# GpSimd behind VectorE's weight operations, by semaphore; and 21 calls of zero products in place of 30

## The chip, the core and the metric

The kernel runs on one core of a Trainium2 chip. A core has TensorE (matmuls, with their results in PSUM), VectorE, ScalarE and GpSimd (elementwise work and reductions), and SyncE, which here issues the transfers between HBM and SBUF. Each engine executes its own instructions in the order in which they are written; between engines, semaphores order them. The metric is the time on the device of one execution in microseconds, lower is better. Three runs of the kernel before took 982.82, 984.07 and 984.09, median 984.07.

## The reference

Rotary attention over 4 batches, 8 heads, 576 positions and head size 64, then two feed-forward blocks over the 2304 tokens:

```
q_rot, k_rot = rotate(q), rotate(k)          # halves turned by cos, sin of the position
scores = q_rot @ k_rot.T / 8;  attn = softmax(scores, axis=-1)
x = attn @ v                                 # (2304, 512)
h = x @ w_in                                 # (512, 2048)
x = where(h > 0, h, exp(min(h, 0)) - 1) @ w_out
out = ((x @ w1) * (x @ w2)) @ w3 @ w_out2    # inner width 1024
```

All is float32. The weights are handed to the kernel as 64-bit words (the float arrives as two 32-bit halves), which three integer operations on VectorE and one on ScalarE make into float32.

## The kernel before, in words

The kernel has three stages, the attention (up to about 280 us of the trace), the first feed-forward block, and the second one with the output. Products are made as three matmuls of split operands (high times high, high times low, low times high; `PAIRS`).

**The attention.** Two heads of a batch are one unit (`units`, 16 of them). A unit goes through five chunks of query rows (`c` from 0 to 4). For each: TensorE multiplies the scores into PSUM (`score`, L406), two buffers (`ps_s`) that alternate; VectorE takes the negative maximum (`most`, L466); ScalarE takes the exponential into SBUF (`expo_s`, L472), which frees the buffer; TensorE turns the result (`half`, L417), VectorE or ScalarE copies it out of PSUM (L481, L479), and TensorE multiplies it by v (`weigh`, L590). The fifth chunk of a unit holds the last 64 rows of both heads (`scores_4`, products with `diag`).

Beside that run preparations. *Rotary steps* for a later unit: for k (640 columns) and q (576) each two products by the table (L330), a sum (L333), a copy of the high part on ScalarE (L82), and the low part (`low`, L339). They may go to GpSimd or VectorE; in the attention after unit 0 all are on GpSimd. `low` frees the buffer for a further load of q or k by SyncE. *Weights* (`weight_steps`): for each of 16 blocks one operation on ScalarE (L124) and three on VectorE, a shift (L127) and two that combine two inputs (L130, L133), on 128 x 512 integers. *Spreads* (L86 on GpSimd, L82 on ScalarE) of 1/sum, which TensorE turns; *sums* of weights on GpSimd (L165 to L168) and at the end of the attention its parts of the next stage's operands (L185, L193, L148).

**The order.** The class `Plan` writes one list for all engines. Each operation has an engine (or a choice of two), a planned duration, a due time and predecessors; `order()` simulates the engines and yields the operations by planned start, and the loop behind `first_scores()` writes them out in this order. TensorE's operations keep the order in which they were added, the others go by due time among those that can start. GpSimd and the VectorE operations with `lock=True` (the three per weight, and VectorE's rotary steps) share one entry in `free`, so that in the plan neither starts before the other's end, less 0.02 us:

```
if e == "pool" or e == "dve" and ops[i][8]:
    t = max(t, free.get("lock", t) - 0.02)
```

That exclusion is in the plan alone. In the program nothing orders a weight operation and a GpSimd operation on other data.

**The start.** `first_load` fetches the table and the first unit's k and q in parts. Meanwhile TensorE multiplies zeros (`warm_up(WARM)`; a call of a float32 product shows as two matmuls in the trace). `first_rope` makes the first operands on VectorE and ScalarE. `first_scores` multiplies the first chunk's scores in two halves, with `warm_up(FILL_IN)` between them; `FILL` puts further such products ahead of later chunks of unit 0.

Of the kernel before, what the change touches and what calls it, by code (L numbers as in the profile page):

```python
# [31 lines left out]
HOLD_0 = 12.0  # L32
AHEAD = dict(act=0.2, dve=0.2, pool=0.3)
RATHER = {"dve/act": dict(act=0.1), "pool/dve": dict(dve=1.2), "pool/act": dict(act=0.3)}
WARM = 30
FILL = (4, 2, 2, 2, 2)
FILL_IN = 4


PRE = [(z, 2 * q + i) for q in range(3) for z in "io" for i in range(2)] + [("o", 6 + i) for i in range(4)]  # L40
# [19 lines left out]
def kernel(  # L60
    ctx: ExitStack, tc: tile.TileContext, q, k, v, tables, ident, w_in, w_out, w1, w2, w3, w_o2, out
):
    nc = tc.nc
    act, dve, pool, pe = nc.scalar, nc.vector, nc.gpsimd, nc.tensor
# [152 lines left out]
    class Plan:  # L217
# [10 lines left out]
        def order(self):  # L228
            ops, done, free, sent = self.ops, {}, {}, {}
            ops = [o[:6] + (max(o[6], o[3] - self.hold),) + o[7:] if o[0] != "pe" else o for o in ops]  # L230
            need = [[self.at[d] for d in o[5] if d in self.at] for o in ops]
            queues = {}
            for i, o in enumerate(ops):
                for e in o[0].split("/"):
                    queues.setdefault(e, []).append(i)
            for e, q in queues.items():
                if e != "pe":
                    q.sort(key=lambda i: ops[i][3])
            line = EARLY
            while any(queues.values()):  # L240
                best = None
                for e, q in queues.items():
                    found = []
                    for i in q[:1] if e == "pe" else q[:120]:
                        if all(d in done for d in need[i]):
                            t = max([free.get(e, self.start[e]), ops[i][6]] + [sent.get(d, done[d]) if e == "sp" else done[d] for d in need[i]])
                            if e == "pool" or e == "dve" and ops[i][8]:
                                t = max(t, free.get("lock", t) - 0.02)
                            found.append((t + (RATHER[ops[i][0]].get(e, 0.0) if "/" in ops[i][0] else 0.0), ops[i][3], i, t))
                    if not found:  # L250
                        continue
                    t0 = min(found)[0]
                    s, _, i, t = min((f for f in found if f[0] <= t0 + AHEAD.get(e, 0.05)), key=lambda f: f[1])
                    if best is None or s < best[0]:
                        best = s, e, i, t
                assert best, [(e, [(list(self.at)[i], [list(self.at)[d] for d in need[i] if d not in done]) for i in q[:6]]) for e, q in queues.items()]
                _, e, i, t = best
                o = ops[i]
                b = o[1][e] if "/" in o[0] else o[1]
                for e_ in o[0].split("/"):  # L260
                    queues[e_].remove(i)
                free[e] = t + b
                if e == "pool" or e == "dve" and o[8]:
                    free["lock"] = free[e]
                if e == "sp":
                    line = max(line, t + 1.5) + o[2]
                    done[i] = line + 0.7
                    if o[7]:
                        sent[i] = t
                else:  # L270
                    done[i] = t + b + o[2]
                f = o[4]
                yield t, (lambda: f(e)) if "/" in o[0] else f, (e, b), i

    ctx_o = ctx.enter_context(ExitStack())
    ctx_x = ctx.enter_context(ExitStack())
# [3 lines left out]
    with ExitStack() as c1:  # L280
# [118 lines left out]
        def score(i, c, e, n, z):  # L399

            hl = hls[units[i]]
            h = slice(64 * e, 64 * e + 64) if c < 4 else slice(0, P)
            a, b = PAIRS[z]
            w = hl[h, a, c * P:c * P + P] if c < 4 else diag[i % 2][:, a]
            at_ = S + 64 * (1 - e) + 288 * n
            pe.matmul(S_t[i, c, e][:, n, :288], w, hl[h, b, at_:at_ + 288], start=(z == 0), stop=(z == 2))  # L406

        def open_s(i, c, e):
            S_t[i, c, e] = ps_s.tile([P, 2, 512], F32, tag="s", name="s")
# [9 lines left out]
        def first_scores():  # L419
            for e in range(2):  # L420
                open_s(0, 0, e)
            for n in range(2):
                if n:
                    warm_up(FILL_IN)
                for z in range(3):
                    for e in range(2):
                        score(0, 0, e, n, z)
# [243 lines left out]
        for i in range(NU):  # L671
            for c in range(5):
                k_ = ("Pb", i, c) if c < 4 else ("S4", i)
                t = nom[k_] + (0.4 if c < 4 else 0.85)
                for e, name in enumerate("ab" if c < 4 else "4"):
                    x = (i, c) if c < 4 else (i,)
# [9 lines left out]
            for c in range(4):  # L686
                k_ = (i, c + 2) if c < 2 else (i + 1, c - 2)
                free = (("PV", i - 1, 0, 1),) if c < 2 else (("PV", i - 1, 1, 2),)
                EV(("evy", i, c), nom["Pa", *k_] + 1.0, lambda e, i=i, c=c: evacuate(i, c, 1, e), ("Pa", *k_), *free)
                EV(("evx", i, c), nom["Pc", *k_] + 1.0, lambda e, i=i, c=c: evacuate(i, c, 0, e), ("Pc", *k_), *free)  # L690
            t = nom["T4", i] + 0.5
            EV(("ev4", i), t + 1.2, lambda e, i=i: evacuate_4(i, e), ("T4", i), ("PV", i - 1, 1, 2))
            t = nom["l1", i] + 0.5
            OP("dve/act", dict(dve=V_(256) + V_(128), act=A_(256, False) + A_(128, False)))(("evl", i, 1), t + 0.8, lambda e, i=i: evacuate_tails(i, 1, e), ("l1", i), ("PV", i - 1, 1, 1))
            t = nom["r1", i] + 0.5
            OP("dve/act", E_(320))(("evr", i, 1), t + 1.5, lambda e, i=i: evacuate_spread(i, 1, e), ("r1", i))
            t = nom["s0", i] + 0.5
            OP("dve/act", E_(256))(("evl", i, 0), t + 0.4, lambda e, i=i: evacuate_tails(i, 0, e), ("s0", i), ("PV", i - 1, 0, 1))
            OP("dve/act", E_(256))(("evr", i, 0), t + 0.8, lambda e, i=i: evacuate_spread(i, 0, e), ("s0", i), ("evl", i, 0))
            for hf in range(2):  # L700
                dep = ("expb", i, 1) if hf == 0 else ("exp4", i)
                t = nom[("s0", i) if hf == 0 else ("r1", i)]
# [3 lines left out]
                t = nom[dep]  # L706
# [28 lines left out]
        for i in range(1, NU):  # L735
            if i:
                t0 = nom["Pa", i, 0]
                for w in (1, 0):
# [4 lines left out]
                    t = t0 - (7.5, 14.5)[w]  # L743
# [15 lines left out]
        for m, (z, f) in enumerate(PRE):  # L759
            key = (z, f)  # L760
            t = AT_0 + 18.0 + (end - AT_0 - 34.0) / (len(PRE) - 1) * m
# [14 lines left out]
        for n in range(SUMS):  # L776
            t = nom["Pa", 8 + 3 * n, 0]
# [17 lines left out]
        t = nom["Pa", NU - 1, 2]  # L795
# [19 lines left out]
        def warm_up(n):  # L815

            ps = ps_t.tile([P, 512], F32, tag="t", name="warm") if n else None
            for _ in range(n):
                pe.matmul(ps[:, :P], warm, warm, start=True, stop=True)
# [10 lines left out]
        dve.memset(warm, 0.0)  # L830
        warm_up(WARM)
        for d in diag:
# [3 lines left out]
        pool.memset(rb[1][:, 2], 0.0)  # L836
        pool.memset(pl1[64:, 256:], 0.0)
        first_scores()
        for t, fn, o, i in plan.order():
            fn()  # L840
            if PLOG is not None:
                PLOG.append((t, o[0], o[1], list(plan.at)[i]))

# [17 lines left out]
    with ExitStack() as c2:  # L861
# [129 lines left out]
        for n in range(N1 + 1):  # L991
            t = T(n)
            p, f = divmod(n, NQ)
# [98 lines left out]
        for n in range(N1):  # L1092
            due = T(n)
            for q in range(4):
                w = (512, 512, 512, 256)[q]
                free = (LAST_USE[(q - 1) % 4], n - 1 if q else n - 2)
# [31 lines left out]
        for n in range(N1):  # L1128
            for z in (1, 0):
# [3 lines left out]
                free = ("Y3", n - 1) if z else ("Y1", n)  # L1133
# [6 lines left out]
        for p in range(1, NT3):  # L1140
            t = T(p * NQ)
# [56 lines left out]
        for m, w in enumerate(every):  # L1198
# [5 lines left out]
            if w[0] == "e":  # L1204
                if w[1][0] == "h" and w[1][2] == 0:
                    f = w[1][1]
# [36 lines left out]
        t = T(N1)  # L1243
        for j in range(8):
            at_ = O_AT[j]
            free = [("wo", N1 - NQ + WO_AT.index(at_), z) for z in range(2)] if at_ in WO_AT else [("made", *w) for w in early[-3:]]
# [305 lines left out]
```

## Time and profile before

| | |
|---|---|
| median of three runs | 984.07 us |
| profiled execution, its own time | 984.18 us |
| span of its trace | 982.4 us |
| TensorE busy | 959.7 us, 98% |
| VectorE busy | 795.1 us, 81% |
| ScalarE busy | 650.4 us, 66% |
| GpSimd busy | 218.6 us, 22%, all of it in the first 276 us |
| mean granted TensorE clock | 0.997 |

A time in the trace counts from its first instruction. Busy is what an engine spent in instructions; TensorE's matmuls are pipelined and their ends are modelled, so a busy TensorE is not one at its peak. PEclk in a stretch is the mean granted clock, 1.00 being 2.4 GHz and 0.50 being 1.2 GHz. PE is TensorE, PEld its loading of the stationary operand, DVE VectorE, ACT ScalarE, POOL GpSimd, SP SyncE. An entry such as `[1.78 <-POOL hl L339]` says that the engine stood idle for 1.78 us before the instruction, and what ended that. A tile's number is left out of its name. A row of stretches has, after its length, the busy microseconds and the number of instructions of PE, PEld, DVE, ACT and POOL, then the clock, the share of the DMA engines and GB/s; a unit's stretch runs from the start of one unit's first product with `diag` to that of the next.

### The profile page before, as it was taken

The numbers are of one execution on the slowest core, as the hardware profiler recorded it, in microseconds if no ns is written. First come the engines' busy times: TensorE is split into PE (matmuls) and PEld (weight loads), VectorE is DVE, ScalarE is ACT, GpSimd is POOL, SyncE is SP. The second block draws the span as 40 slices with busy tenths as digits, with TensorE's granted clock in tenths as the row PEclk, the third lists the DMA queues.
The fourth block names the chain that finished last, engine by engine and source line by source line (L and its number), as shares of the span: only waits on it lengthen the run. The fifth ranks groups of instructions, "written<-read, shape, count | busy, mean of one in ns | idle before, by whom it ended". The sixth has DMA issues, their size and how long they took to land.

```text
span 982.4 us, 17951 instructions
## 1 busy us (share of the span) xinstructions
PE 959.7 (98%) x6652; PEld 833.0 (85%) x6652; DVE 795.1 (81%) x1499; ACT 650.4 (66%) x1393; POOL 218.6 (22%) x190
## 2 busy tenths in 40 slices
PE   8899999999999999999999999999999999999998
PEld 7676676666779999999999999988899999999997
DVE  5899899999879999999999999847656666676444
ACT  4687787767778787888788877865344444444342
POOL 4999998886510000000000000000000000000000
PEclk9999999999999999999999999999999999999999
DMA  6444443442403356476655676614232342224201
GB/s 212 162 145 138 147 130 138 153 136 79 165 3 116 122 192 205 160 229 226 193 188 155 196 246 202 220 44 150 66 95 76 87 139 76 75 91 147 81 27 64
DMA packets 62536, 134.54 MB, mean 137 GB/s; under 512 B 6640, under 2 KB 15472, under 8 KB 62448
## 3 DMA queue, kind: packets, MB, share of 16 engines
q1 hardware_dynamic: 62448, 133.39, 42.3%
q8 instruction: 52, 0.85, 0.3%
q14 instruction: 36, 0.29, 0.1%
HBM read 107.68 MB, written 25.69 MB: 136 GB/s over the span
## 4 chain that ended last, share of the span: by engine, by line
PE 71%; DVE 3%; ACT 1%; DMA 1%; issue 1%; ACTq 0%; DVEq 0%
PE y L923 12%; PE A L1353 10%; PE o L1379 10%; PE A L880 9%; PE B L1353 7%; PE B L880 7%; PE yb L924 6%; PE w L1283 4%; PE o L590 2%; PE s L406 2%; DMA set<-kept 1%; PE ptp L417 1%; DVE set L141 0%; DVE xc L78 0%; ACT pr L472 0%
## 5 line engine op out<-in xcount | busy, mean ns | idle before, releaser
L923 PE MATMUL y<-g,wo 128*128 128x512 f32 x576 | 204.1, 392 | 0.0
L924 PE MATMUL yb<-g,wo 128*128 128x256 f32 x576 | 161.2, 280 | 0.0
L141 DVE TENSOR_TENSOR set<-set 128x512 fp32r<-128x512 f32 (+1 forms) x160 | 98.2, 619 | 40.4 <-ACT set L138 40.2
L406 PEld LDWEIGHTS s<-hl 64*128 64x128 f32 x768 | 86.9, 185 | 46.3 <-ACT pr L472 32.4
L472 ACT ACTIVATE pr<-s,nm 128x576 f32<-128x576 f32 x144 | 105.5, 738 | 31.1 <-DVE nm L466 30.1
L923 PEld LDWEIGHTS y<-g,wo 128*128 128x128 f32 x576 | 107.8, 187 | 20.4
L406 PE MATMUL s<-hl 64*128 64x288 f32 x768 | 108.8, 315 | 12.8 <-ACT pr L472 10.9
L1353 PE MATMUL A<-xc,set 128*128 128x384 f32 x576 | 116.1, 336 | 0.2
L466 DVE TENSOR_REDUCE nm<-s 128x1 f32<-128x576 f32 x144 | 102.7, 748 | 12.2 <-PE s L406 11.9
L880 PE MATMUL A<-xf,set 128*128 128x384 f32 x552 | 111.2, 336 | 0.8 <-ACT p L937 0.7
L1379 PE MATMUL o<-W,g 128*128 128x512 f32 x432 | 111.1, 393 | 0.0
L1353 PEld LDWEIGHTS A<-xc,set 128*128 128x128 f32 x576 | 102.3, 188 | 7.8 <-DVE p L1440 1.0
L924 PEld LDWEIGHTS yb<-g,wo 128*128 128x128 f32 x576 | 108.7, 189 | 0.1
L880 PEld LDWEIGHTS A<-xf,set 128*128 128x128 f32 x552 | 93.7, 188 | 4.1 <-ACT p L937 1.4
L82 ACT ACTIVATE g<-p 128x384 fp32r<-128x384 f32 x48 | 25.2, 525 | 107.8 <-DVE p L1440 71.5
L330 POOL TENSOR_TENSOR raw_qk<-raw_qk,tab 128x640 f32<-128x640 f32 (+1 forms) x60 | 90.7, 1523 | 3.2 <-DMA raw_qk<-q_ 2.9
L1379 PEld LDWEIGHTS o<-W,g 128*128 128x128 f32 x432 | 80.0, 188 | 12.7
L138 ACT ACTIVATE set<-set 128x512 fp32r<-128x512 f32 (+1 forms) x160 | 89.3, 567 | 1.9 <-DMA set<-kept 1.7
L1353 PE MATMUL B<-xc,set 128*128 128x384 f32 x432 | 86.5, 334 | 0.0
L417 PE MATMUL ptp<-idt,pr 64*128 64x64 f32 x1024 | 86.3, 226 | 0.0
L880 PE MATMUL B<-xf,set 128*128 128x384 f32 x420 | 84.3, 336 | 0.0
L417 PEld LDWEIGHTS ptp<-idt,pr 64*128 64x128 f32 x1024 | 76.9, 139 | 0.9 <-DVE nm L466 0.5
(248 smaller groups left out, 1833.7 us busy)
## 6 DMA issues: line engine op xcount, KB each, us to landing
set<-kept SPq DMA_DIRECT2D x120, 256.0 KB, 2.8
raw<-w_ SPq DMA_DIRECT2D x32, 512.0 KB, 4.1
kept<-wr SPq DMA_DIRECT2D x40, 256.0 KB, 3.2
raw_qk<-k_ SPq DMA_DIRECT2D x15, 640.0 KB, 5.5
raw_qk<-q_ SPq DMA_DIRECT2D x15, 576.0 KB, 4.7
raw<-w_in_ SPq DMA_DIRECT2D x16, 512.0 KB, 5.8
raw<-w_out_ SPq DMA_DIRECT2D x16, 512.0 KB, 5.0
w<-kept SPq DMA_DIRECT2D x24, 256.0 KB, 3.1
```

Of the source, the lines that this page charges most:

```text
L138: act.activation(t[:, 0, :w], t[:, 1, :w].bitcast(F32), ACTF.Copy)
L141: eng.tensor_tensor(t[:, 1, :w], t[:, 1, :w].bitcast(F32), t[:, 0, :w].bitcast(F32), op=ALU.subtract)
L330: eng.tensor_tensor(r[:, z], r[:, z], tab[:, w, z, TAB[w]], op=ALU.mult)
L406: pe.matmul(S_t[i, c, e][:, n, :288], w, hl[h, b, at_:at_ + 288], start=(z == 0), stop=(z == 2))
L417: pe.transpose(pts[i, c, z][:, e, kc], pr[h, at_:at_ + P], idt[h, h])
L466: dve.tensor_reduce(nm_t[i, c, e], S_t[i, c, e][:, :, :288], axis=AX.XY, op=ALU.max, negate=True)
L472: act.activation(pr_t[i, c][:, e].rearrange("p (n i) -> p n i", n=2), S_t.pop((i, c, e))[:, :, :288], ACTF.Exp, bias=nm_t.pop((i, c, e)), ...
L880: pe.matmul(banks[b][:, :HF], set_w(n, k, a, c), x[:, e, c], start=(start and i == 0), stop=i == 5, skip_group_check=True,)
L923: pe.matmul(y_t[p, o], w_, g[:, c, :512], start=s, stop=t, skip_group_check=True)
L924: pe.matmul(yb_t[p, o // 2][:, o % 2], w_, g[:, c, 512:], start=s and o % 2 == 0, stop=t, skip_group_check=True,)
L1353: pe.matmul(ps[:, :HB], w[:, a, c * P:(c + 1) * P], x[:, c, b], start=(start and i == 0), stop=i == 5, skip_group_check=True,)
L1379: pe.matmul(outs[p, o], g[:, a, o % 3 * P:o % 3 * P + P], wW[f][:, c], start=(f == 0 and i == 0), stop=(f == NG - 1 and i == 2),)
```

## The change

The plan's exclusion is written as two rules without the 0.02 us: a GpSimd operation starts no earlier than the end of the last locked VectorE operation (`BEHIND[0]` is added, 0.0), and a locked VectorE operation no earlier than the end of the last GpSimd operation (`BEHIND[1]`, 0.0). `order()` also yields whether an operation is locked.

In the loop that writes the list out, the last instruction of each locked VectorE operation is remembered. The first GpSimd instruction of the next GpSimd operation in the list is then made dependent on it, so it waits by semaphore for that VectorE instruction's end. One GpSimd operation waits, those behind it follow in GpSimd's own order. No wait is added on VectorE.

Apart from that, `WARM` goes from 30 calls to 21 and `FILL_IN` from 4 to 6.

```diff
--- before.py
+++ after.py
@@ -32,9 +32,10 @@
 HOLD_0 = 12.0
 AHEAD = dict(act=0.2, dve=0.2, pool=0.3)
 RATHER = {"dve/act": dict(act=0.1), "pool/dve": dict(dve=1.2), "pool/act": dict(act=0.3)}
-WARM = 30
+BEHIND = (0.0, 0.0)
+WARM = 21
 FILL = (4, 2, 2, 2, 2)
-FILL_IN = 4
+FILL_IN = 6
 
 
 PRE = [(z, 2 * q + i) for q in range(3) for z in "io" for i in range(2)] + [("o", 6 + i) for i in range(4)]
@@ -244,8 +245,10 @@
                     for i in q[:1] if e == "pe" else q[:120]:
                         if all(d in done for d in need[i]):
                             t = max([free.get(e, self.start[e]), ops[i][6]] + [sent.get(d, done[d]) if e == "sp" else done[d] for d in need[i]])
-                            if e == "pool" or e == "dve" and ops[i][8]:
-                                t = max(t, free.get("lock", t) - 0.02)
+                            if e == "pool":
+                                t = max(t, free.get("by_dve", t) + BEHIND[0])
+                            if e == "dve" and ops[i][8]:
+                                t = max(t, free.get("pool", t) + BEHIND[1])
                             found.append((t + (RATHER[ops[i][0]].get(e, 0.0) if "/" in ops[i][0] else 0.0), ops[i][3], i, t))
                     if not found:
                         continue
@@ -260,8 +263,8 @@
                 for e_ in o[0].split("/"):
                     queues[e_].remove(i)
                 free[e] = t + b
-                if e == "pool" or e == "dve" and o[8]:
-                    free["lock"] = free[e]
+                if e == "dve" and o[8]:
+                    free["by_dve"] = free[e]
                 if e == "sp":
                     line = max(line, t + 1.5) + o[2]
                     done[i] = line + 0.7
@@ -270,7 +273,7 @@
                 else:
                     done[i] = t + b + o[2]
                 f = o[4]
-                yield t, (lambda: f(e)) if "/" in o[0] else f, (e, b), i
+                yield t, (lambda: f(e)) if "/" in o[0] else f, (e, b, o[8]), i
 
     ctx_o = ctx.enter_context(ExitStack())
     ctx_x = ctx.enter_context(ExitStack())
@@ -836,8 +839,21 @@
         pool.memset(rb[1][:, 2], 0.0)
         pool.memset(pl1[64:, 256:], 0.0)
         first_scores()
+        behind = None
         for t, fn, o, i in plan.order():
+            traced = nc.cur_bb.bb.instructions
+            n = len(traced)
             fn()
+            if o[0] == "pool" and behind:
+                mine = [x for x in nc.cur_bb.bb.instructions[n:] if x.engine == behind[1]]
+                if mine:
+                    tc.add_manual_dep(
+                        mine[0], behind[0], mybir.DependencyInfo(mybir.DependencyClass.Sync, mybir.DependencyReason.DATA),
+                        reason="behind",
+                    )
+                    behind = None
+            elif o[0] == "dve" and o[2]:
+                behind = nc.cur_bb.bb.instructions[-1].name, mybir.EngineType.Pool
             if PLOG is not None:
                 PLOG.append((t, o[0], o[1], list(plan.at)[i]))
```

## Rows read from the trace of the kernel before

**Rows 1.** Stretches, one per unit: length, busy us of each engine, TensorE clock
```profile
26.69:44.31 17.62, 15.67 (x169) 11.17 (x167) 14.81 (x26) 13.05 (x31) 15.50 (x14) 0.90 0.42 149
...
124.25:140.03 15.78, 15.38 (x178) 10.94 (x174) 14.08 (x28) 13.18 (x33) 13.85 (x12) 1.00 0.42 139
...
188.49:203.81 15.32, 15.14 (x175) 10.90 (x173) 14.04 (x28) 11.92 (x30) 14.52 (x14) 1.00 0.41 142
203.81:222.12 18.31, 15.88 (x173) 10.99 (x173) 17.30 (x29) 12.22 (x32) 13.60 (x11) 1.00 0.45 149
...
238.82:254.24 15.42, 15.19 (x173) 10.92 (x174) 15.01 (x32) 10.95 (x26) 5.48 (x8) 1.00 0.09 28
...
sum 243.14, PE 231.22 PEld 164.35 DVE 221.74 ACT 184.71 POOL 203.04; mean PE 15.41 PEld 10.96 DVE 14.78 ACT 12.31 POOL 13.54
```

**Rows 2.** Waits, 28 to 262 us: who, releaser, total us, times, longest
```profile
PEld s L406 <- ACT pr L472: 30.5, 54, 2.1
ACT pr L472 <- DVE nm L466: 24.9, 30, 1.7
```

**Rows 3.** Groups on VectorE, 28 to 262 us: busy us, mean ns, idle before
```profile
L133 DVE SCALAR_TENSOR_TENSOR pair<-raw,pair 128x512 int32<-128x512 int32 x16 | 17.8, 1112 | 0.0
L130 DVE SCALAR_TENSOR_TENSOR pair<-raw,pair 128x512 int32<-128x512 int32 x16 | 14.9, 930 | 0.0
L127 DVE TENSOR_SCALAR pair<-pair 128x512 int32<-128x512 int32 x16 | 14.0, 873 | 0.0
```

**Rows 4.** Single lines, whole kernel: least/median/most ns, first and last start
```profile
L127 DVE TENSOR_SCALAR pair<-pair x32: 384/420/1709, 29.9 to 375.6; 128x512 int32<-128x512 int32 x32
L130 DVE SCALAR_TENSOR_TENSOR pair<-raw,pair x32: 654/684/2027, 34.0 to 380.5; 128x512 int32<-128x512 int32 x32
L133 DVE SCALAR_TENSOR_TENSOR pair<-raw,pair x32: 658/685/1934, 37.4 to 383.0; 128x512 int32<-128x512 int32 x32
```

**Rows 5.** Timeline, GpSimd beside VectorE, two pairs: start us, duration us, what
```profile
53.26 2.12 POOL L333 TENSOR_TENSOR raw_qk<-raw_qk 128x576 f32<-128x576 f32 x1
53.43 0.68 DVE L130 SCALAR_TENSOR_TENSOR pair<-raw,pair 128x512 int32<-128x512 int32 x1
...
204.07 1.55 POOL L330 TENSOR_TENSOR raw_qk<-raw_qk,tab 128x640 f32<-128x640 f32 x1
204.14 2.03 DVE L130 SCALAR_TENSOR_TENSOR pair<-raw,pair 128x512 int32<-128x512 int32 x1
```

**Rows 6.** Timeline: last rotary step (units 2, 7), first score (unit 2)
```profile
42.84 1.40 POOL L339 TENSOR_TENSOR hl<-raw_qk,hl 128x576 fp32r<-128x576 f32 x1
46.52 0.40 PE L406 MATMUL s<-hl 64*128 64x288 f32 x1
...
109.52 3.39 POOL L339 TENSOR_TENSOR hl<-raw_qk,hl 128x640 fp32r<-128x640 f32 x2
```

**Rows 7.** Timeline, 0 to 30 us; in brackets idle before, releaser
```profile
1.04 9.81 PE L819 MATMUL warm<-warm 128*128 128x128 f32 x60 [1.04 <-DVE warm L830]
...
8.88 0.43 DVE L375 SCALAR_TENSOR_TENSOR hl<-raw_qk,hl 128x256 fp32r<-128x256 f32 x1
...
11.42 0.89 DVE L359 TENSOR_TENSOR raw_qk<-raw_qk,tab 128x320 f32<-128x320 f32 x2
...
13.17 0.76 DVE L466 TENSOR_REDUCE nm<-s 128x1 f32<-128x576 f32 x1 [0.87 <-PE s L406]
...
15.19 0.49 DVE L375 SCALAR_TENSOR_TENSOR hl<-raw_qk,hl 128x320 fp32r<-128x320 f32 x1 [0.19 <-ACT hl L82]
...
15.76 0.65 POOL L86 TENSOR_SCALAR diag<-hl 64x128 fp32r<-64x128 f32 x2 [13.57 <-DVE hl L375]
...
19.26 0.69 ACT L124 ACTIVATE pair<-raw 128x512 f32<-128x512 f32 x1 [0.41 <-DMA raw<-w_in_]
...
29.84 0.18 PEld L406 LDWEIGHTS s<-hl 64*128 64x128 f32 x1 [1.78 <-POOL hl L339]
```

**Rows 8.** Two microseconds of the products of zeros; columns as in rows 1
```profile
8.00:10.00 2.00, 2.00 (x20) 2.00 (x19) 1.95 (x5) 0.42 (x1) 0.00 (x0) 1.00 1.02 385
```

## The prediction

> **What bounds the kernel now.** I read the busy shares by stage first (only the attention, up to about 280 us, has GpSimd at work, and there TensorE idles), then cut the attention into its 16 units, which are the period of its list. The cuts are the starts of the products with `diag` that close a unit. A unit is 16.21 us on the mean (243.14 / 15), but units 7, 11 and 14 take 15.78, 15.32 and 15.42, mean 15.51, and unit 12 takes 18.31 [rows 1]. The long unit is long on VectorE: 17.30 us busy with 29 instructions, against 14.04 with 28 in unit 11, while TensorE has the same 173 to 178 matmuls in each. The waits tell how that reaches TensorE: scores wait for the exponentials that free their PSUM buffer (30.5 us), and the exponentials wait for the maxima on VectorE (24.9 us) [rows 2]. VectorE executes in the order of its list, so whatever delays one of its instructions delays the next maximum.
>
> What delays it are the three operations per weight. 16 of each form run in the attention with means of 873, 930 and 1112 ns [rows 3]; the same forms have medians of 420, 684 and 685 ns over all 32, the half behind the attention included, where GpSimd is silent [rows 4]. The excess is 16 x (0.453 + 0.246 + 0.427) = 18.0 us. One of them can be watched: GpSimd starts a rotary product at 204.07, VectorE its operation at 204.14, and this takes 2.03 us, 1.35 over its median, ending 0.55 behind the product's end at 205.62 [rows 5].
>
> I went through all 48 operations so, with the list in hand: 19 of them carry 16.2 of the 18.0 us, and in each of these the GpSimd operation that held VectorE up stands behind the weight operation in the list and ran past it. The other 1.8 us come from GpSimd operations that stand ahead of it.
>
> **The waits.** 44 of the 48 weight operations have a GpSimd operation behind them before the next weight operation; the last few, where GpSimd has little to do, share one. So some 44 waits are added, all on GpSimd. Behind a waiting instruction stand the rest of GpSimd's list: rotary steps, whose last one (`low`, L339) the next unit's scores need, the spreads of 1/sum (L86), which the turned sums on TensorE need, and two sums of weights. SP's loads of q and k wait for `low` too.
>
> What VectorE gets back: the 19 stalls, 16.2 / 18.0 = 0.9 of the excess, if nothing comes in their place. What that is worth is read from the units, not from 18.0 us: leaving out unit 1 and the three undisturbed ones, 11 units take 243.14 - 17.62 - 46.52 = 179.0 us, against 11 x 15.51 = 170.6. So 8.4 us of the attention's length go with the stalls. The rest of the 18.0 us is covered already (VectorE has room in most units).
>
> What GpSimd pays: in 21 pairs the later operation started before its weight operation would have ended; summed over them (weight operation's start plus its unblocked time, minus GpSimd's start) it is 24.7 us, over 44 waits 0.56 each. The hand-over adds 0.08 us, as from VectorE's end at 15.19 + 0.49 = 15.68 to GpSimd's start at 15.76 [rows 7]. So about 0.6 us per wait, three waits a unit. GpSimd's own pace is read from `low` of q: it ends at 44.24 for unit 2 and for unit 7, as the second of the row's two operations, at 109.52 + 3.39 = 112.91: 68.67 / 5 = 13.73 us a unit [rows 6]. With 3 x 0.6 it is 15.5, just the undisturbed pace of TensorE. It fits with no room, and the slack at the beginning is small: unit 2's `low` ends at 44.24 and its first score runs at 46.52 [rows 6].
>
> So not all of it is gained. Where VectorE comes early, it now meets the GpSimd operation ahead of it in the list; where it comes late, GpSimd stands and its next operations are late. I let a third of the gain go for that: 8.4 x 0.9 x 2/3 = 5.0 us, between 0 (every stall comes back from the operation ahead) and 8.4; below nothing only by GpSimd as pacemaker, below. I lean to the upper half since the list itself is written as if the two excluded each other, so a wait in it mostly restores the order that was meant.
>
> A rule of the Trainium skill (SBUF — State Buffer, section "Who interferes with whom") says that an operation with two SBUF inputs and a GpSimd operation that reads SBUF take one port pair in turn, and the second to start is blocked for the whole of the first. The 2.03 us of rows 5 agree; in the other pair there GpSimd begins at 53.26, VectorE 0.17 later, and yet VectorE runs its plain 0.68 us while the add on GpSimd takes 2.12, against 1.40 for an operation of its size in rows 6. So within 0.2 us the starts do not tell the winner. By the rule taken alone a wait only picks the loser and the gain would be 0.
>
> Unit 1 is 17.62 us, 2.1 over, but its TensorE also stood 1.78 us for `low` at 29.84 [rows 7] and ran at a mean granted clock of 0.90, so partly at 1.2 GHz [rows 1]. Of its 2.1 I take 0.3, between 0 and 2.1.
>
> **The plan's arithmetic.** The old form let either engine start 0.02 us before the other's end, the new one does not. That can turn single choices of order; I cost it at 0 and leave ±1 us for it, about a unit's usual scatter (15.32 to 15.78 undisturbed).
>
> **The products of zeros.** 30 calls are 60 matmuls from 1.04 to 10.85 [rows 7]. Nine calls fewer are 18 matmuls at the end of the row, where 20 stand in 2.00 us [rows 8]: 1.8 us, so they end at about 9.05. The first scores' last operand is there at 8.88 + 0.43 = 9.31. They run then some 1.5 us earlier, and two more calls of filling put back 4 x 0.10 = 0.4 us before the second half. The maximum that began at 13.17, 0.87 us idle before it, can start when VectorE is free: 11.42 + 0.89 = 12.31 [rows 7]. That is 0.86 us. But ScalarE already waited 0.41 us for a weight's load at 19.26 [rows 7], and a load does not come earlier with TensorE; exponentials stand behind it. GpSimd's chain, which sets 29.84, does not pass there until it needs ScalarE's high parts. I take 0.4 us, between 0 and 0.86. The clock rose while the old products ran and 42 are left of 60, so I expect it to rise at the same time.
>
> **Sum.** 5.0 + 0.3 + 0.4 = 5.7 us. Behind the attention nothing changes, and its first products wait for TensorE's own last ones, so the gain is kept. The profiled execution took 984.18 us, its span 982.4 and 1.8 around it; that is 0.1 above the median. 984.18 - 5.7 = 978.5, and against the median 978.4.
>
> **Rivals.**
> *GpSimd becomes the pacemaker* (slower). Today's units leave it (16.21 - 13.73) / 3 = 0.83 us per wait. Beyond that every unit from 2 on waits for `low`. At 1.0 us a unit is 16.73: 0.52 x 13 units = 6.8, less the 2.3 us of slack: +4.5, about 988. For it: the small slack in units 2 and 3, and the spreads, which stand in GpSimd's line. Against it: 0.6 is what the pairs give, and the slack is larger from unit 5 on.
> *The stall changes sides* (about the same). VectorE, now earlier, meets the operation ahead each time and loses as much as before. Only the start's 0.4 is left: 983.7. For it: the rule above; half of a 1.55 us operation is 0.78, more than today's mean of 18.0 / 48 = 0.375. Against it: each wait also brings the two back into step.
> *All of it comes back*: 8.4 + 2.1 + 0.86 = 11.4 us, 972.7. Against it: GpSimd's 15.5 us a unit.
> *The waits don't do it*: the list turns out in another order, with the stalls elsewhere: 984 ± 3.
>
> **Chances.** Forecast (975.5 to 981.5) 0.55; all of it 0.08; changes sides 0.17; pacemaker 0.12; another order 0.08. A difference of under 0.2%, 2.0 us, cannot be told from no change here. Faster: 0.55 + 0.08 + 0.05 of the changed sides + 0.04 of the other order = 0.72; same 0.14; slower 0.12 + 0.02 = 0.14. For 8 in 10 the range takes the forecast, most of the changed sides and the nearer part of the full gain: 974.5 to 985.
>
> **What would show it.** Right: the three weight operations fall to means under 0.75 us in the attention, GpSimd's waits name `pair` of VectorE, units come to 15.5 to 15.9, the first maximum starts near 12.3. Wrong: GpSimd's `low` is what scores wait for in units 2 to 6 (pacemaker), or the means of rows 3 stay while the GpSimd operation that blocks is the one ahead (changed sides), or the start's gain is gone at 19.26.

## The result, and the profile after

The changed kernel takes 973.99 us (median of four runs, 972.47 to 975.60) against 983.87 for the kernel before, measured beside it (median of four, 982.82 to 984.09): 0.9902 of it, interval 0.9880 to 0.9923. I had forecast 978.4 and a range down to 974.5. The direction is right, and the gain is 9.9 us instead of 5.7.

The profiled execution took 972.47 us, its span is 970.7. The stretches of the units, cut as in [rows 1] and with the same columns:

```profile
25.83:42.08 16.25, 14.11 (x168) 10.46 (x166) 13.65 (x26) 12.37 (x30) 14.55 (x12) 1.00 0.41 150
...
119.81:135.11 15.30, 15.29 (x173) 11.00 (x174) 14.68 (x29) 11.65 (x28) 13.44 (x15) 1.00 0.44 144
...
181.55:196.81 15.26, 15.09 (x174) 10.90 (x174) 13.71 (x30) 12.16 (x29) 13.50 (x13) 1.00 0.40 143
196.81:212.74 15.93, 15.56 (x173) 10.99 (x173) 14.62 (x28) 12.70 (x33) 13.55 (x11) 1.00 0.49 171
...
228.21:243.55 15.34, 15.16 (x174) 10.90 (x174) 15.05 (x32) 11.22 (x26) 5.48 (x9) 1.00 0.08 27
...
sum 232.94, PE 227.14 PEld 163.41 DVE 216.39 ACT 181.25 POOL 197.61; mean PE 15.14 PEld 10.89 DVE 14.43 ACT 12.08 POOL 13.17
```

Here the difference of the two spans, 982.4 - 970.7 = 11.7 us, can be shared out. Unit 1 now ends at 42.08 instead of 44.31: 2.2 us. Units 2 to 15 take 232.94 - 16.25 = 216.69 instead of 243.14 - 17.62 = 225.52: 8.8 us. The rest behind the attention gives 0.6, which is scatter (it lies between 710.9 and 713.5 us in the fourteen profiles of this study). Unit 12, which was 18.31, is 15.93: VectorE is busy for 14.62 us in it instead of 17.30, with one instruction less. The medians over all fifteen units are no longer pulled up by a few long ones.

The waits that answer to [rows 2], 28 to 262 us, and the largest groups of the new ones, on GpSimd (who, releaser, total us, times, longest):

```profile
PEld s L409 <- ACT pr L475: 24.9, 57, 1.1
ACT pr L475 <- DVE nm L469: 12.8, 18, 1.5
...
POOL rb L87 <- DVE ri L560: 5.4, 3, 3.4
...
POOL xs L186 <- DVE pair L134: 5.3, 1, 5.3
POOL raw_qk L333 <- DVE pair L131: 5.0, 8, 0.6
...
POOL hl L342 <- DVE pair L128: 2.6, 3, 1.7
POOL rb L87 <- DVE pair L131: 2.5, 4, 0.6
POOL raw_qk L333 <- DVE pair L134: 2.5, 4, 0.6
POOL raw_qk L333 <- DVE pair L128: 2.4, 5, 0.9
...
PEld s L409 <- POOL hl L342: 1.4, 1, 1.4
```

The exponentials wait half as long for maxima (12.8 us instead of 24.9). GpSimd now waits for `pair`, mostly for 0.4 to 0.9 us at a time; one of the waits ahead of `low` (`hl`, L342) takes 1.7 us, and the one of 5.3 us stands at the end of the attention, ahead of the next stage's operands (L186). The scores wait for GpSimd's `low` once, in unit 1, as before.

The weight operations that answer to [rows 3]:

```profile
L131 DVE SCALAR_TENSOR_TENSOR pair<-raw,pair 128x512 int32<-128x512 int32 x16 | 15.2, 950 | 0.0
L134 DVE SCALAR_TENSOR_TENSOR pair<-raw,pair 128x512 int32<-128x512 int32 x16 | 14.5, 907 | 0.0
L128 DVE TENSOR_SCALAR pair<-pair 128x512 int32<-128x512 int32 x16 | 9.7, 607 | 0.0
```

Against the medians of [rows 4] 16 x (0.266 + 0.222 + 0.187) = 10.8 us of excess are left of 18.0. So the operations are still held up, and yet most of the time is gained. Which ones are left is seen in a stretch of VectorE and GpSimd (start, duration, idle before):

```profile
72.67 1.56 POOL L336 TENSOR_TENSOR raw_qk<-raw_qk 128x640 f32<-128x640 f32 x1
...
73.07 1.71 DVE L131 SCALAR_TENSOR_TENSOR pair<-raw,pair 128x512 int32<-128x512 int32 x1
...
74.86 1.41 POOL L333 TENSOR_TENSOR raw_qk<-raw_qk,tab 128x576 f32<-128x576 f32 x1 [0.63 <-DVE pair L131]
```

GpSimd's operation of 72.67 stands ahead of the weight operation in the list, VectorE comes 0.40 us after it began and stands until 0.55 us behind its end: the picture of [rows 5], with the other neighbour. The next GpSimd operation waits and starts 0.08 us after VectorE's end, 73.07 + 1.71 = 74.78. In all 48 operations, with undisturbed times of 0.40, 0.67 and 0.67 us, what is left comes from a GpSimd operation ahead, none from one behind. Before, 12 of them were held up for more than 0.8 us each, 13.6 us together; now 2, with 2.1 us.

The start, answering to [rows 7]:

```profile
1.04 6.33 PE L822 MATMUL warm<-warm 128*128 128x128 f32 x42 [1.04 <-DVE warm L833]
...
8.56 0.86 PE L409 MATMUL s<-hl 64*128 64x288 f32 x6 [1.19 <-ACT hl L83]
...
11.88 0.75 DVE L469 TENSOR_REDUCE nm<-s 128x1 f32<-128x576 f32 x1
...
18.40 0.67 ACT L125 ACTIVATE pair<-raw 128x512 f32<-128x512 f32 x1 [0.84 <-DMA raw<-w_in_]
...
28.61 0.18 PEld L409 LDWEIGHTS s<-hl 64*128 64x128 f32 x1 [1.43 <-POOL hl L342]
```

The first maximum starts at 11.88 instead of 13.17, ScalarE waits 0.43 us longer for its weight's load than before, and the scores that wait for `low` go on at 28.61 instead of 29.84.

### The profile page after: what moved, and what is told of

It reads as the page before. It is cut to its first block, busy times and chain, and to the rows that moved or that the text cites. A ratio compares the mean times of both kernels' runs of the same rounds, so it can differ in the third digit from the quotient of the medians.

```text
span 970.7 us, 17968 instructions
## 1 busy us (share of the span) xinstructions
PE 953.1 (98%) x6638; PEld 829.1 (85%) x6638; DVE 789.8 (81%) x1507; ACT 647.2 (67%) x1378; POOL 213.6 (22%) x197
## 4 chain that ended last, share of the span: by engine, by line
PE 73%; DVE 3%; ACT 1%; DMA 0%; issue 0%; ACTq 0%; DVEq 0%; SPq 0%
PE y L939 13%; PE A L1369 10%; PE o L1395 10%; PE A L896 9%; PE B L1369 8%; PE B L896 7%; PE yb L940 7%; PE w L1299 5%; PE o L593 2%; PE s L409 2%; PE ptp L420 1%; DVE set L142 0%; DVE xc L79 0%; DVE e L970 0%; DVE wr L131 0%
## 5 line engine op out<-in xcount | busy, mean ns | idle before, releaser
L409 PE MATMUL s<-hl 64*128 64x288 f32 x768 | 106.5, 314 | 6.4 <-ACT pr L475 4.0
L333 POOL TENSOR_TENSOR raw_qk<-raw_qk,tab 128x640 f32<-128x640 f32 (+1 forms) x60 | 88.5, 1484 | 10.7 <-DVE pair L131 5.0
```

What stands on the lines that cost most here:

```text
L333: eng.tensor_tensor(r[:, z], r[:, z], tab[:, w, z, TAB[w]], op=ALU.mult)
```

## The experiments

The change has three parts: the waits, the list without its 0.02 us (another list: of the 396 VectorE operations that the plan of before had in the attention 340 stand in matching order in the new one, of 295 on ScalarE 247, of 158 on GpSimd 126), and the start. E1 to E4 take them one by one. Times are given as ratios to the kernel before on the same chip; beside them stands the length of units 2 to 15 of the profiled run, which neither the start nor the clock touches, except where said. In the views below the columns are those of [rows 1].

**E1, the new list alone.**

```diff
-WARM = 21
+WARM = 30
...
-FILL_IN = 6
+FILL_IN = 4
...
             fn()
-            if o[0] == "pool" and behind:
...
-                behind = nc.cur_bb.bb.instructions[-1].name, mybir.EngineType.Pool
```

> The list of the changed kernel (the plan's exclusion without the 0.02 us), no waits, products of zeros as before (30 and 4 calls). Theory A, the waits bring the gain: 982 to 986, the weight operations keep means some 0.35 us over their medians, GpSimd runs past them again. Theory B, the other list brings it (it gives ScalarE's and VectorE's copies out and the rotary steps in another order): 975 to 979, with the stalls still there. Theory C, the start and the clock bring it: 983.5 to 984.5.

1.0017 (1.0006 to 1.0029), some 1.7 us slower. Units 2 to 15 of E1:

```profile
43.63:269.74 226.11, 214.67 (x2422) 153.00 (x2423) 210.14 (x393) 169.33 (x400) 191.77 (x161) 1.00 0.42 137
```

226.11 us, 0.6 more than before, which is within the scatter of a list without waits (E3 below). By itself the new list gives nothing.

**E2, the waits alone**, on the list of before and with its start. Against the changed kernel (`WARM` and `FILL_IN` as in E1):

```diff
...
-                            if e == "pool":
-                                t = max(t, free.get("by_dve", t) + BEHIND[0])
-                            if e == "dve" and ops[i][8]:
-                                t = max(t, free.get("pool", t) + BEHIND[1])
+                            if e == "pool" or e == "dve" and ops[i][8]:
+                                t = max(t, free.get("lock", t) - 0.02)
...
-                if e == "dve" and o[8]:
-                    free["by_dve"] = free[e]
+                if e == "pool" or e == "dve" and o[8]:
+                    free["lock"] = free[e]
...
```

> The waits on the list of before, products of zeros as before. Theory A: 976 to 979, weight operations no longer passed, their excess of 18.0 us down to some 11 as in the changed kernel. Theory B: 982 to 985, since the list of before then only moves its stalls to the GpSimd operation ahead. Theory C: 983 to 984.5.

0.9946 (0.9930 to 0.9961): 5.3 us. Units 2 to 15 of E2:

```profile
44.91:264.98 220.07, 215.38 (x2422) 153.27 (x2423) 204.36 (x385) 172.53 (x414) 179.09 (x154) 1.00 0.43 141
```

225.52 - 220.07 = 5.45 us. The excess of the weight operations fell only from 18.8 to 15.3 us (by the undisturbed times above), but the stalls of over 0.8 us went from 12 to 3.

**E3, the start alone.**

```diff
-WARM = 30
+WARM = 21
...
-FILL_IN = 4
+FILL_IN = 6
```

> 21 and 6 calls of zeros in place of 30 and 4, the list and the missing waits of before. Theory A and theory B: 983 to 984, a gain of 0.4 to 0.9. Theory C: 980 to 982, with the stretch at 1.2 GHz in unit 1 (3.4 us in the trace of before) gone.

0.9986 (0.9977 to 0.9995): 1.4 us. This run also tells how far one list scatters without the waits. Its list is that of the kernel before, and its units 2 to 15 take 224.36 us against 225.52; unit 9 takes 15.78 against 16.94. The excess of its weight operations is 15.1 us, no more than with the waits of E2, but 10 of its stalls last over 0.8 us, against 3 there.

**E4, list and waits, with the start of before.** Its edit against the changed kernel is that of E1 in `WARM` and `FILL_IN` alone.

> List and waits of the changed kernel, products of zeros as before. Theories A and B, and that the two only work together: 974.5 to 976, the start's share being 0.4 to 0.9. Theory C: 977 or more, and a stretch at 1.2 GHz in unit 1.

0.9910 (0.9893 to 0.9926): 8.9 us. Units 2 to 15 of E4 and of the changed kernel built once more, which ran as E9:

```profile
44.84:261.54 216.70, 213.01 (x2422) 152.87 (x2422) 202.81 (x393) 168.80 (x400) 183.06 (x161) 1.00 0.44 144
```

```profile
44.59:261.32 216.73, 213.04 (x2422) 152.84 (x2423) 202.81 (x393) 168.81 (x400) 183.08 (x161) 1.00 0.43 144
```

With the waits the list is executed alike each time: 216.69, 216.70 and 216.73 us. From E2 to E4 only the list differs: 3.6 us in the times, 220.07 - 216.70 = 3.4 us in the units. So the same list costs 1.7 us without the waits and gives 3.6 with them.

**E5 and E6, both lists without any conflict.** There are no waits, and in place of the three operations per weight VectorE reduces the same raw tile; 16 weights are not made. E5 has the list of before, E6 that of the changed kernel, both with the start of before.

```diff
+        def reduced(n):
+            return lambda: dve.tensor_reduce(scr, r[:, :n], axis=AX.X, op=ALU.max)
+        if key in PRE:
+            return rebase, reduced(320), reduced(512), reduced(512)
         return rebase, shift, low, sign
```

> The list of before without waits; the three operations of each weight in the attention are replaced by reductions of the same length in time (320, 512 and 512 columns, one input in SBUF), so those 16 weights are not made. The question is what a unit takes when nothing holds VectorE up. Theory B1, the old list has a floor of its own at some 15.5 us a unit, where the prediction put it: 233 us from the first to the last diag product, 974 us, and the reductions stay within 0.1 us of their plain time. Theory B2, the stalls are all there is and both lists have one floor at 15.25: 229 us. If reductions stall like the weights' own operations, neither is told and the port does not depend on two inputs.

> The same with the list of the changed kernel, without waits; the 16 weights are not made. Theory B1, the new list is the better one by itself and the stalls hid it: 15.2 to 15.25 us a unit, 229 us over fifteen, some 4 us below the old list in the same form. Theory B2: the two come out within 1 us of each other.

E5 0.9913 (0.9890 to 0.9936), E6 0.9904 (0.9879 to 0.9930). Their reductions of 512 columns, which read one operand from SBUF (the line is the same in both runs), and units 2 to 15, for E5 and then for E6:

```profile
L138 DVE TENSOR_REDUCE scr<-pair 128x1 f32<-128x512 f32 x32 | 21.5, 673 | 0.0
...
43.12:260.34 217.22, 214.49 (x2422) 153.09 (x2422) 193.26 (x386) 171.48 (x414) 176.76 (x153) 1.00 0.43 144
```

```profile
45.94:260.73 214.79, 212.37 (x2423) 152.81 (x2423) 194.75 (x393) 168.08 (x400) 180.66 (x161) 1.00 0.44 145
```

All 32 reductions of 512 columns take 673 ns on the mean, the longest 686, beside a GpSimd that executes as many instructions as ever (153 in units 2 to 15 of E5 and of the kernel before): no stall. GpSimd is not held up either, 176.76 us busy there instead of 187.54. So these are the floors of the two lists, by one profile of each: 217.22 / 14 = 15.52 us a unit for the old one, 15.34 for the new one. The new one is 2.4 us lower; the expectation for it had been some 4. Of what the conflicts cost over that floor, the waits take 5.45 of 225.52 - 217.22 = 8.3 us on the old list, and 9.4 of 226.11 - 214.79 = 11.3 us on the new one. (E6's time hides part of its floor, since TensorE ran at a mean granted clock of 0.78 in its unit 1.)

**E7, E8 and E12, other margins in the plan, with the waits and the new start.** They are the changed kernel but for the two numbers.

```diff
-BEHIND = (0.0, 0.0)
+BEHIND = (0.1, 0.0)
```

This is E7; E8 has (0.02, 0.02), E12 (-0.1, -0.05).

> The changed kernel with another list: BEHIND = (0.1, 0.0), so the plan grants GpSimd 0.1 us for the hand-over that the trace shows (0.08). Theory B, the rewritten list is better because it has no overlap and grants the wait: 972 to 975. Theory L, which list comes out is a matter of chance worth several us either way: anything from 972 to 982, and as good or bad as its units' floor.

> The changed kernel with BEHIND = (0.02, 0.02), another list again, the margin as far on the other side of zero as the old one was. Theory B: 973 to 976, as the changed kernel. Theory L: off by several us, more likely slower, 976 to 984, since the plan of this list ends later.

> The changed kernel with BEHIND = (-0.1, -0.05): another list, whose planned end is as early as the changed kernel's (0.05 us later; the two lists before it planned 1.4 and 7.2 us later and came out at 974.1 and 980.3). Theory L1, lists differ by chance and the plan does not tell: 972 to 981. Theory L2, the plan's own end tells a good list from a bad one once the waits hold it to the plan: 972 to 976.

| list | planned end, us | ratio (interval) | units 2 to 15, us | excess of the 48, us | of it in stalls over 0.8 us (how many) |
|---|---|---|---|---|---|
| of before, no waits | 272.8 | 1 | 225.52 | 18.8 | 13.6 (12) |
| of before, no waits, new start (E3) | 272.8 | 0.9986 (0.9977 to 0.9995) | 224.36 | 15.1 | 11.1 (10) |
| changed, no waits (E1) | 271.5 | 1.0017 (1.0006 to 1.0029) | 226.11 | 19.8 | 14.4 (12) |
| of before, waits (E2) | 272.8 | 0.9946 (0.9930 to 0.9961) | 220.07 | 15.3 | 2.6 (3) |
| changed | 271.5 | 0.9902 (0.9880 to 0.9923) | 216.69 | 11.6 | 2.1 (2) |
| E7 | 272.9 | 0.9899 (0.9878 to 0.9920) | 218.23 | 8.4 | 1.1 (1) |
| E8 | 278.7 | 0.9960 (0.9947 to 0.9973) | 223.78 | 8.0 | 1.9 (2) |
| E12 | 271.6 | 0.9935 (0.9919 to 0.9950) | 222.05 | 15.5 | 4.8 (5) |

Lists that differ by margins of a tenth of a microsecond or less lie up to 6 us apart, with the same waits. The excess of the weight operations does not sort them (E8 has the least and is the slowest of those with waits), and neither does the planned end (E12 plans what the changed kernel plans). On one and the same list, E3 and E2 have the same excess and lie 4.3 us apart; what the waits changed there is the long stalls. In E8 one unit takes 19.25 us, and its rows show a list that is bad in itself: five weight operations in a row on VectorE, none of them held up, ahead of the maximum that the exponentials, and through them the scores, wait for.

```profile
160.06 0.68 DVE L134 SCALAR_TENSOR_TENSOR pair<-raw,pair 128x512 int32<-128x512 int32 x1
160.66 0.47 DVE L128 TENSOR_SCALAR pair<-pair 128x512 int32<-128x512 int32 x1
161.16 0.69 DVE L131 SCALAR_TENSOR_TENSOR pair<-raw,pair 128x512 int32<-128x512 int32 x1
161.89 0.69 DVE L134 SCALAR_TENSOR_TENSOR pair<-raw,pair 128x512 int32<-128x512 int32 x1
162.50 0.42 DVE L128 TENSOR_SCALAR pair<-pair 128x512 int32<-128x512 int32 x1
162.83 0.75 DVE L469 TENSOR_REDUCE nm<-s 128x1 f32<-128x576 f32 x1
```

Behind that the clock adds to it. These are two stretches of the same unit:

```profile
162.00:164.00 2.00, 0.41 (x4) 0.00 (x0) 2.00 (x4) 0.38 (x1) 0.94 (x1) 1.00 0.87 301
...
166.00:168.00 2.00, 2.00 (x17) 1.67 (x17) 1.77 (x5) 1.07 (x2) 1.90 (x2) 0.50 0.37 145
```

TensorE is busy for 0.41 of 2 us while it waits, and from 165.47 on its granted clock is 0.50 for 3.41 us. What of the 19.25 us is the list's and what the clock's is not told apart.

**E11, waits in both directions.** A weight operation now also waits for the GpSimd operation ahead of it in the list.

```diff
-        behind = None
+        behind = ahead = None
...
             elif o[0] == "dve" and o[2]:
+                if ahead:
+                    mine = [x for x in nc.cur_bb.bb.instructions[n:] if x.engine == mybir.EngineType.DVE]
+                    tc.add_manual_dep(mine[0], ahead, ...)
+                    ahead = None
                 behind = nc.cur_bb.bb.instructions[-1].name, mybir.EngineType.Pool
+            if o[0] == "pool":
+                mine = [x for x in nc.cur_bb.bb.instructions[n:] if x.engine == mybir.EngineType.Pool]
+                ahead = mine[-1].name if mine else ahead
```

> The changed kernel with waits in both directions: a weight operation on VectorE also waits by semaphore for the GpSimd operation ahead of it in the list. Theory P, in the changed kernel VectorE is already held there by GpSimd in all of the remaining stalls, so the semaphore only names the same wait: within 1 us of the changed kernel, the operations back at 0.39 to 0.69 us and the wait shown as idle time behind GpSimd. Rival, the hand-over costs on VectorE each time, 48 x 0.08 us in VectorE's line: 2 to 4 us slower.

0.9967 (0.9954 to 0.9979), 7.4 us slower than the changed kernel beside it (E9), which neither expectation had. The groups on VectorE (busy us, mean ns, idle before):

```profile
L134 DVE SCALAR_TENSOR_TENSOR pair<-raw,pair 128x512 int32<-128x512 int32 x16 | 11.1, 691 | 7.1 <-POOL rb L87 2.9 <-POOL raw_qk L333 1.9 <-POOL raw_qk L336 1.8
L131 DVE SCALAR_TENSOR_TENSOR pair<-raw,pair 128x512 int32<-128x512 int32 x16 | 11.1, 691 | 7.8 <-POOL raw_qk L336 2.4 <-POOL rb L87 1.8 <-POOL hl L342 1.6
L128 DVE TENSOR_SCALAR pair<-pair 128x512 int32<-128x512 int32 x16 | 6.8, 424 | 4.3 <-POOL hl L342 1.4 <-POOL raw_qk L333 1.2 <-POOL raw_qk L336 1.0
```

The operations are as short as behind the attention, but VectorE stands ahead of them for 4.3 + 7.8 + 7.1 = 19.2 us, more than the 11.6 us that the stalls took. One such wait on VectorE:

```profile
33.82 1.54 POOL L336 TENSOR_TENSOR raw_qk<-raw_qk 128x640 f32<-128x640 f32 x1
...
35.39 0.69 DVE L131 SCALAR_TENSOR_TENSOR pair<-raw,pair 128x512 int32<-128x512 int32 x1 [0.75 <-POOL raw_qk L336]
```

It starts 0.03 us behind GpSimd's end (33.82 + 1.54 = 35.36) and ends 0.72 behind it; the stalled operation at 73.07 in the changed kernel ended 0.55 behind its neighbour. VectorE waits so in 40 of the 48 operations, and in 32 of these GpSimd was already at work when VectorE came. That is 0.72 - 0.55 = 0.17 us later each time, and 40 x 0.17 = 6.8 us, an estimate from these rows, is near the 7.4. A stall that is left alone is the cheaper wait on this engine.

**E9 and E10, the changed kernel again, and with more products of zeros in units 0 and 1.** TensorE has room there, and in some executions of the changed kernel its granted clock falls.

```diff
-FILL = (4, 2, 2, 2, 2)
+FILL = (4, 2, 2, 6, 8)
...
-                    PE(("warm", c), 0.1, lambda c=c: warm_up(FILL[c]))
+                    PE(("warm", c), 0.1, lambda c=c: warm_up(FILL[c], "t" if c < 3 else "o"))
+                if (i, c) == (1, 0):
+                    PE(("warm", 5), 0.0, lambda: warm_up(6, "o"))
...
```

> The changed kernel itself once more, beside the next three on one chip. All theories: 972 to 976. If a stretch at 1.2 GHz around 20 to 35 us is what spreads its runs, runs with a mean clock of 1.0 stand near 972.6 and runs at 0.993 near 975.4, as in its first four.

> The changed kernel with more products of zeros where TensorE idles in unit 0 and before unit 1 (FILL of 6 and 8 calls in place of 2 and 2 ahead of the chunks 3 and 4, 6 more ahead of unit 1), in the PSUM buffer of the weighted values, which is free until then. Theory K, the stretch at 1.2 GHz comes from TensorE's idling in 20 to 29 us and costs 2 to 3 us when it comes: all runs at a mean clock near 1.0, 971.5 to 973.5. Rival, the stretch comes whatever TensorE does there, or the new products delay the scores: 973 to 977.

E9: 974.28 us, 0.9893 (0.9875 to 0.9911). E10: 972.46 us, 0.9872 (0.9852 to 0.9892), the fastest kernel of the study; its four runs lie between 972.31 and 973.17. Two stretches of E9 and the same of E10:

```profile
20.00:25.00 5.00, 2.44 (x32) 1.88 (x32) 3.41 (x6) 3.58 (x10) 4.92 (x5) 0.98 0.07 10
25.00:30.00 5.00, 4.24 (x22) 3.42 (x22) 1.29 (x3) 1.67 (x5) 4.12 (x3) 0.50 0.56 215
```

```profile
20.00:25.00 5.00, 4.26 (x52) 3.67 (x49) 3.33 (x6) 3.58 (x9) 5.00 (x4) 1.00 0.04 12
25.00:30.00 5.00, 4.28 (x41) 4.02 (x39) 2.92 (x8) 2.95 (x8) 4.92 (x4) 1.00 0.62 223
```

In E9 TensorE is busy for 2.44 of 5 us and then stands at a granted clock of 0.50, which is 1.2 GHz, for 10.2 us from 24.82 on; unit 1 takes 18.07 us instead of 16.25. In E10 it is busy for 4.26 us and the mean granted clock is 1.0 in all four runs, against two of the nine runs of the changed kernel. Its first four sort by it: 972.47 and 972.76 us at a mean granted clock of 1.0, 975.22 and 975.60 at 0.993. So the stretch costs some 2.8 us when it comes. The gap alone does not bring it each time: in the changed kernel's own profile TensorE is busy for 2.43 us between 20 and 25 us, and the clock stays.

## Why the prediction was wrong in size

**The waits: right in size, in part by luck.** I took 5.0 us. E2 gives 5.3 by its time and 5.45 by its units. The 8.4 us and the undisturbed unit of 15.51 us under it hold: E5 has 8.3 and 15.52. Three good units of one trace were enough for the floor. The two thirds of it were a guess, and the reason I gave for them is not what happened. I let a third go because some stalls would come back from the GpSimd operation ahead; in E2 nearly all came back. GpSimd operations behind the weight operation in the list held VectorE up for 16.2 us before and for none in E2, those ahead for about 2 before and for 14.9 in E2. The gain came although the excess fell by only 3.5 us; what went is the long stalls.

**The plan's arithmetic: this step failed.** The prediction put it so: "That can turn single choices of order; I cost it at 0 and leave ±1 us for it". With the waits it is worth 3.6 us (E2 against E4), which is nearly the whole miss: 978.4 - 3.6 = 974.8. By the runs the sum is 5.3 + 3.6 + 0.8 (the start, below) = 9.7 of the 9.9 us. The choices turned were not single; the lists part within the second unit and then differ through the whole attention. 2.4 us of it are a lower floor (E5, E6), the rest is less loss to conflicts above the floor (E2 has 220.07 - 217.22 = 2.9 us of that, the changed kernel 216.69 - 214.79 = 1.9). That another list came out as a gain is luck: E8 and E12, with margins as small and the new start, gain nothing over E2 and its start of before (0.9960 and 0.9935 against 0.9946, where the start is worth 0.0014). I had read the scatter of single units, 15.32 to 15.78, as the bound of the step, but it adds up over 14 units: 14 x 0.18 = 2.5. What makes that floor lower is not shown. In E6 ScalarE has 400 instructions in units 2 to 15 and in E5 414, busy 168.1 and 171.5 us, and the exponentials run on ScalarE; that this is the cause is only argued, and no run moved that work alone.

**The start: right in kind, too small.** I took 0.4 for it and 0.3 for unit 1. E3 gives 1.4 (0.5 to 2.3), E4 against the changed kernel some 0.8, or 1.7 by the changed kernel's second measurement (E9). The trace of the changed kernel, with no stretch at 1.2 GHz, has unit 1 end 2.2 us earlier, E9, with one, 0.3 us later (44.59 against 44.31). So this term has two values, and a median lies between them. The first maximum came at 11.88, earlier than the 12.3 expected: the 42 products of zeros ended at 7.37, not at 9.05, as TensorE's rate had risen sooner in this execution (20 products between 4 and 6 us, 11 in the kernel before); I had expected it to rise at the same time. That 0.43 us more of waiting for the load at ScalarE give part of it back was as expected.

**GpSimd as pacemaker: not seen.** I had set 13.73 + 3 x 0.6 = 15.5 us a unit. The price of a wait was right: in the view of waits above and its smaller groups GpSimd stands 19.6 us in 32 waits for `pair` without the last one, 0.61 each. What failed is the adding. GpSimd's waits before, 28 to 262 us, were these:

```profile
POOL rb L86 <- DVE ri L557: 14.4, 12, 4.9
POOL hl L339 <- ACT hl L82: 13.5, 13, 5.2
```

After, the first is 5.4 us (L87 on L560) and the second is not among its waits: the 19.6 us of new ones stand where 22.5 us of old ones were. `low` of q ends at 41.56 for unit 2 and at 114.13 for unit 7 in the changed kernel, 14.5 us a unit, a microsecond under TensorE's 216.69 / 14 = 15.5.

**The stall changes sides: half true, and cheap.** All that is left comes from the operation ahead, as that rival had it, and the means of L131 and L134 stay above the 0.75 us that I had set as a sign. But what remains costs 216.69 - 214.79 = 1.9 us, not all of the gain. The long stalls are gone (2 over 0.8 us instead of 12), and VectorE's room in a unit covers short ones. That length decides is read from the last two columns of the table, above all from E3 against E2, and not tried by itself.

**The rule of the Trainium skill.** The Trainium skill (SBUF — State Buffer, section "Who interferes with whom") has the operation that starts second blocked for the whole of the first. Its mechanism agrees with what is seen here: each remaining stall begins behind a GpSimd operation already running, as the 1.71 us at 73.07. By the same section of the Trainium skill a reduction with one SBUF input does not contend with GpSimd, and E5 agrees (673 ns). I had drawn from the rule that a wait only picks the loser, for a gain of 0. What does not follow from it is the price: which of the two stands matters for the time (E2 gains 5.3 us). That this is because the two engines have different things queued behind them is argued from the lists, not tried. E11, which lets both stand, loses 7.4 us.

## What to carry to other kernels

A change to the numbers of a list scheduler is an edit of its own: build the list with and without it and price the two lists apart, since neither the planned end nor the stalled time told here which was faster, and 0.02 us in a rule was worth 3.6. Where two engines hold each other up, count the long stalls apart from the short ones. Let the engine wait that has room, and leave the other to stall; price the wait by what the waiting engine waited for anyway, not by adding it to its pace. Where a term can come out two ways from run to run, as a clock that falls in an idle stretch, look for the cheap work that keeps it from falling (E10) ahead of any further tuning.

## What the runs showed of the hardware that was not expected

- Without the waits the same list is executed in different ways: units 2 to 15 of the list of before took 225.52 and 224.36 us. With them four profiles of the new list (changed kernel, E4, E9, E10) lie between 216.69 and 216.73.
- In units 0 and 1 every profile but those of the changed kernel and of E10 has a stretch at 1.2 GHz, the shortest of 3.41 us (kernel before), the longest of 13.65 us (E6). E8 has a second one in the middle of the attention, at 165.47, behind the wait of TensorE shown above.
- The hand-over from VectorE to GpSimd by the added semaphore took 0.08 us (74.78 to 74.86), as the one in [rows 7] did; the one from GpSimd to VectorE in E11 took 0.03 us (35.36 to 35.39).
